# Sums of the output projection over 128 partitions, and kv joined with the next batch's projections, in a fused attention-and-FFN kernel

## The chip, the cores and the metric

The kernel runs on one core of one Trainium2 chip, in fp32. The metric is the device time of one execution in microseconds (us). The core's engines run side by side and wait for each other by semaphores: PE (TensorE, matrix products), ACT (ScalarE), DVE (VectorE), POOL (GpSimd) and SP (SyncE, which here only issues DMAs).

## The reference

An attention with squared sketches as features is followed by a gated feed-forward network. The attention's output is its input.

```python
batch, n_heads, seq, head_dim = (4, 4, 1088, 32); r = 8
def phi(x):
    a = np.einsum('rd,bhsd->bhsr', S1, x)
    b = np.einsum('rd,bhsd->bhsr', S2, x)
    return np.einsum('bhsi,bhsj->bhsij', a, b).reshape(*x.shape[:-1], r * r)
q_p, k_p = (phi(q), phi(k))
kv = np.einsum('bhsf,bhsd->bhfd', k_p, v)
z = np.sum(k_p, axis=2)
num = np.einsum('bhsf,bhfd->bhsd', q_p, kv)
den = np.einsum('bhsf,bhf->bhs', q_p, z)[..., None] + 1e-06
x = (num / den).transpose(0, 2, 1, 3).reshape(B * S, H * D)   # 4352 x 128
gate = 1.0 / (1.0 + np.exp(-(x @ w_gate)))                    # 128 -> 1536
return gate * (x @ w_val) @ w_out                             # 1536 -> 128
```

## The kernel before

**The feed-forward network in slots.** The 4352 tokens are cut into nine chunks of 512 (the last has 256). The 1536 hidden columns are twelve blocks of 128. One *slot* of the program handles one block of one chunk, in the last chunk two blocks, so slots are numbered through: slots 0 to 11 are the first chunk, 12 to 23 the second. In a slot, `w1` multiplies the tokens by a block of `w_gate` and `w_val` (a *wave*: eight matmuls, line 540) into one of two PSUM buffers "wave". ACT takes the sigmoid (`sg`, line 548), and at the beginning of the next slot `glu` has DVE multiply (`g`, line 583). The buffer is free for the wave after next when `g` is written. Where a wave buffer is also taken by an attention group (`qcomp`, `parts`), the ring moves by one.

**Seven products instead of eight.** In the seven full chunks after the first, two blocks of `g` (a pair: an even and an odd slot) are multiplied by `w_out` in the manner of Strassen and Winograd: the token dimension is halved (HALF = 256), `token_sums` (line 367, on POOL) forms differences `t[:, 0..3]` of the quarters of the pair, `weight_sums` (line 363) once those of the weights (`ws`), and seven products of 64×256 (`product`, line 377) take the place of eight. Two products run side by side on the two column halves of TensorE. For an odd slot n, `w2_a` with four products is due in slot n+3 and `w2_b` with three in slot n+4. They accumulate over the six pairs of a chunk in two PSUM banks, `acc0` and `acc1`, one for each function. After the sixth pair the partial sums are added: ACT copies what a sum needs from PSUM (lines 473 and 502), DVE adds (`add`, line 479) and transposes (line 514), SP stores.

**The queues of the order.** `moe["todo"]` holds the products with the slot in which they are due; `moe["late"]` holds closing work of a chunk, of which `slot()` takes one item per slot behind `glu`. Then come the products that are due, and then `w1`. The order of PE, DVE, ACT and POOL is the order in which the program is written; that of the DMA issues on SP is set by a scheduler. An engine does its instructions in that order.

**The attention between the slots.** Batch 0 and the first weights are handled ahead of and in the first slots. The work of batches 1 to 3 is put between slots by hand; for 2 and 3, `plan` lists the slot of each step:

- `turn_k`, `turn_q` (DVE transposes), then in `begin` the projections `kps` of k and `qcomp` of q (TensorE), whose result `spread` writes to DRAM and reads back spread over the partitions into `qp`, `bq`, and in small pieces `a` and `b` (SP).
- `outer` (DVE, the features of k, line 752), `sum_z` (DVE, lines 926 ff.), `kv` (TensorE, 36 small matmuls at line 892 and four at 901) and its copy `kvd` (ACT, line 914).
- `weights_z` (three DVE instructions from line 1001), `ndt` (line 957), `qmult` (DVE, the features of q, line 872), and `parts`: `den_j` (line 1021), numerators `nps` (line 1258), `den_i` (line 1034), whose quotient goes into `xT`, the tokens of the next waves.

`kps`, `kvz` and the second part of the numerators, `nps2`, take turns in one PSUM buffer "two". `load_kq` and `load_v` load the inputs of a batch. `kq` and `bq` take turns in buffers of the pool `ld`.

Of the kernel before, what the change touches and what calls it, by code (L numbers as in the profile page):

```python
# [8 lines left out]
F32 = mybir.dt.float32  # L9
# [7 lines left out]
P = 128  # L17
# [3 lines left out]
def kernel(  # L21
# [34 lines left out]
    sbN = ctx.enter_context(tc.tile_pool(name="sbN", bufs=1))  # L56
    sbG = ctx.enter_context(tc.tile_pool(name="sbG", bufs=3))

# [207 lines left out]

    def new_kq(b):
        t = ld.tile([P, 2 * H * W1], F32, tag="kq", name="kq")
        kq = t[:, : 2 * T * D].rearrange("p (a t d) -> p a t d", a=2, t=T)
        k_t[b], q_t[b] = kq[:, 0], kq[:, 1]  # L270
# [76 lines left out]
    moe = {"sum": -1, "ci": 0, "w": 0, "n": 0, "ready": 0, "acc": None, "gate": None, "todo": [], "late": []}  # L347
# [17 lines left out]
    def token_sums(g, t, odd):  # L365
        def sub(u, in0, in1):
            nc.gpsimd.tensor_tensor(out=t[:, u], in0=in0, in1=in1, op=ALU.subtract)  # L367

        if not odd:
            sub(0, g[:, 0, HALF:], g[:, 0, :HALF])  # L370
            return
        sub(2, g[:, 1, HALF:], t[:, 0])
        sub(3, t[:, 2], g[:, 1, :HALF])
        sub(1, g[:, 1, HALF:], g[:, 0, HALF:])

    def product(out, lhsT, rhs, start, stop):
        nc.tensor.matmul(  # L377
            out=out, lhsT=lhsT, rhs=rhs, start=start, stop=stop, skip_group_check=True
        )
# [34 lines left out]
    def w2(ci, j0, jn, g):  # L414
        if j0 == 0:
            moe["sum"] = ci
            moe["acc"] = pso.tile([P, TCH], F32, tag="acc0", name="moeout")
        for jj in range(jn):
            j = j0 + jj
            for d in (slice(0, P),) if j < NJ - 2 else (slice(0, 64), slice(64, P)):  # L420
                nc.tensor.matmul(  # L421
                    out=moe["acc"][d],
                    lhsT=w_sb[:, 2, j, d],
                    rhs=g[:, jj],
                    start=(j == 0),
                    stop=(j == NJ - 1),
                )
        if j0 + jn == NJ:
            o_sb = sbA.tile([P, 2, TCH // 32, 32], F32, tag="o_sb", name="o_sb")[:, 0]
            nc.vector.transpose(out=o_sb.rearrange("p t d -> p (t d)"), in_=moe["acc"])  # L430
            moe["store"] = lambda: store(
                ci, lambda g4: o_sb[32 * g4 : 32 * g4 + 32], nc.scalar
            )
# [25 lines left out]

    def w2_a(ci, i, g, t):  # L460
        if i == 0:
            moe["sum"] = ci
            fst["a"] = pso.tile([P, TCH], F32, tag="acc0", name="prod")
        lo, hi = fst["a"][:64], fst["a"][64:]
        w, first, last = w_sb[:, 2], i == 0, i == NJ // 2 - 1
        product(lo[:, :HALF], w[:, 2 * i, :64], g[:, 0, :HALF], first, last)
        product(hi[:, :HALF], w[:, 2 * i + 1, :64], g[:, 1, :HALF], first, last)
        product(lo[:, HALF:], ws[:, 3, i], g[:, 1, HALF:], False, last)
        product(hi[:, HALF:], ws[:, 1, i], t[:, 2], False, last)
        if last:  # L470
            e = fst["e"] = raw.tile([P, 2, 2, HALF], F32, tag="w_in", name="other")[:64]
            r = fst["r"] = raw.tile([P, 6, HALF], F32, tag="w_in", name="res")[:64]
            nc.scalar.copy(out=e[:, 0], in_=hi.rearrange("p (u x) -> p u x", u=2))

            add(ends(r, 1, 3), twice(lo[:, :HALF]), e[:, 0])
            moe["late"] += [lambda: add(r[:, 2], lo[:, HALF:], r[:, 4])]

    def add(out, in0, in1, op=ALU.add):
        nc.vector.tensor_tensor(out=out, in0=in0, in1=in1, op=op)  # L479

    def twice(x):
        return bass.AP(tensor=x.tensor, offset=x.offset, ap=[list(x.ap[0]), [0, 2], [1, HALF]])

    def ends(r, u, step):
        x = r[:, u]
        return bass.AP(
            tensor=x.tensor, offset=x.offset, ap=[list(x.ap[0]), [step * HALF, 2], [1, HALF]]
        )

    def w2_b(ci, i, g, t):  # L490
        if i == 0:
            fst["b"] = pso.tile([P, TCH], F32, tag="acc1", name="prod")
        lo, hi = fst["b"][:64], fst["b"][64:]
        w, first, last = w_sb[:, 2], i == 0, i == NJ // 2 - 1
        p5 = (lo[:, :HALF], ws[:, 0, i], t[:, 0], first, last)
        p4 = (hi[:, :HALF], w[:, 2 * i + 1, 64:], t[:, 3], first, last)
        p7 = ((hi if i % 2 else lo)[:, HALF:], ws[:, 2, i], t[:, 1], False, i >= NJ // 2 - 2)
        for p in (p4, p5, p7) if i % 2 else (p5, p4, p7):
            product(*p)
        if last:  # L500
            e, r = fst["e"], fst["r"]
            nc.scalar.copy(out=e[:, 1], in_=hi.rearrange("p (u x) -> p u x", u=2))
            o_sb = sbA.tile([P, 2, TCH // 32, 32], F32, tag="o_sb", name="o_sb")

            def fifth_seventh():
                add(ends(r, 2, 3), twice(lo[:, :HALF]), ends(r, 2, 2))
                add(r[:, 0], lo[:, HALF:], e[:, 1, 1])

            def last_sums():
                add(r[:, 3], r[:, 4], e[:, 1, 0], op=ALU.subtract)  # L510
                add(r[:, 3:5], ends(r, 3, 2), twice(r[:, 0]))

            def turned(d):
                nc.vector.transpose(  # L514
                    out=o_sb[:64, d].rearrange("p t x -> p (t x)"),
                    in_=r[:, 1 + 2 * d : 3 + 2 * d].rearrange("p u x -> p (u x)"),
                )

            def turn_store():
                turned(1)  # L520
                store(ci, lambda g4: o_sb[32 * (g4 % 2) : 32 * (g4 % 2) + 32, g4 // 2])

            moe["late"] += [fifth_seventh, last_sums, lambda: turned(0), turn_store]

    def w1():
# [40 lines left out]
        if ci == 1 and j0 == 1:  # L566
            weight_sums(NJ // 4, NJ // 2)
# [4 lines left out]
        def glu():  # L572
# [19 lines left out]
            if odd:  # L592
                part = (ci, j0 // 2, pair, moe["t"])
                early = ci == len(tok_chk) - 2 and j0 == NJ - 1
                todo.append((n + 3 - early, lambda: w2_a(*part)))
                todo.append((n + 4 - early, lambda: w2_b(*part)))
# [13 lines left out]
    def slot(group, waves, behind=None):  # L610
# [4 lines left out]
        for _ in range(waves):  # L615
# [12 lines left out]
            if more:  # L628
                w1()
            elif not todo:  # L630
                break
            else:
                todo.pop(0)[1]()
# [29 lines left out]
    def kps(b):  # L663
        t = ps2.tile([P, 2, 512], F32, tag="two", name="kps")
        ts = [t[:, 0], t[:, 1]]
# [168 lines left out]
    def spread(b, ns, cq, put, get):  # L834
# [19 lines left out]
        B8[b] = sbA.tile([P, W1], F32, tag="b8", name="b8", bufs=1)  # L854
        A8[b] = sbA.tile([P, 2, WD], F32, tag="a8", name="a8", bufs=1)
# [32 lines left out]
    def kv(b, zsum):  # L888
        kvz = KVZ[b] = ps2.tile([P, 2, 512], F32, tag="two", name="kvz")[:, 0]
# [264 lines left out]
    warm(64)  # L1154
# [77 lines left out]
    def begin(b):  # L1232
        glu()
        kps(b)
        cq[b] = qcomp(b, (0, 1), (psm, "wave"))
        spread(b, (0, 1), cq[b], nc.scalar, nc.sync)
# [7 lines left out]
    def part01(first):  # L1244
        glu()
        late.append(dn(0, 1)(first=first, later=True))
# [19 lines left out]
    def parts(b):  # L1266
# [6 lines left out]
        nc.scalar.copy(out=num, in_=t)  # L1273
        t = ps2.tile([P, 2, 512], F32, tag="two", name="nps2")
        numerators(b, t[:, :, WD : WD + 32], True)
        turn_den(b, den_i(b, t[:, 0, :WD]))
        for n in range(2):
# [33 lines left out]
    slot(lambda: part01(lambda: narrow_w(NJ - 1, 3)), 1)  # L1311
    slot(last01, 1)
    load_v(1)
    turn_k(1)
# [19 lines left out]
    load_kq(2)  # L1334
# [7 lines left out]
    plan = {2: (27, 29, 30, 31, 32, 34, 36, 37, 38, 39, 42, 44)}  # L1342
    plan[3] = (48, 49, 51, 53, 56, 57, 58, 59, 60, 61, 63, 68)
    for b in range(2, B):
        at = iter(plan[b])
        until(next(at))
        turn_k(b)
        for n in range(2):
            until(next(at))
            turn_q(b, n)  # L1350
        until(next(at))
        slot(lambda: begin(b), 1)
        for pi in range(2):
            until(next(at))
            outer(b, pi)
        for step in range(2):
            until(next(at))
            sum_z(b, step)
        until(next(at))
        slot(lambda: kv_all(b), 1)  # L1360
        if b + 1 < B:
            load_v(b + 1)
        until(next(at))
        qmult(b, 0)
        slot(lambda: ndt(b), 1)
        weights_z(b)
        until(next(at))
        qmult(b, 1)
        load_kq(b + 1)
        until(next(at))  # L1370
        slot(lambda: parts(b), 1)
# [31 lines left out]
```

## Time and profile before

| | |
|---|---|
| median of 3 runs | 292.99 us (292.74 to 293.36) |
| profiled execution | 296.02 us; span 294.1 us |
| granted TensorE clock | 0.999 of full |
| busy PE / DVE / POOL / ACT | 288.8 / 186.5 / 160.6 / 93.7 us |
| waves, line 540 | 820 matmuls, 210.6 us |
| products, line 377 | 588 matmuls, in four groups of 62.8, 34.7, 25.3 and 25.0 us |
| sums of the products on DVE, line 479 | 35 instructions, 24.9 us; transposes at line 514: 14, 9.6 us |
| token sums on POOL, line 367 | 168 instructions, 134.8 us |

The profile is of one execution and its times are in us; the span is from the first to the last instruction, and the execution's time is 1.92 us more. An engine's busy time says how long it had work, not that anything waited for it. Ends of matmuls are modelled, so the distance between two starts is the safer reading. Matmuls on two halves of the array run side by side, so their busy times add up to more than the engine's. In a line of the timeline stand the start, the duration, the engine, the line of the program, the operation, output and inputs by name, and in square brackets the idle time of the engine just before, with what ended it; a number behind x at the end is that of instructions joined in the line. In the groups, the output's and the input's partitions and elements are given as 128x256.

### The profile page before, as it was taken

What the parts mean: (1) busy time and instruction counts of PE and PEld (TensorE: products, weight loads), DVE (VectorE), ACT (ScalarE), POOL (GpSimd) and SP (SyncE); (2) the same over time, 40 slices, a digit from 0 to 9 for tenths busy, and PEclk for the clock granted to TensorE, in tenths of its full rate; (3) what the DMA queues carried; (4) which work ended last, traced back from release to release, by engine and by line L of the source; (5) the groups of instructions that cost most, each with busy time, mean ns of one, the idle gap of its engine ahead of it and who ended that gap; (6) DMA issues with size and microseconds to landing.
All of it is one profiled execution on the core that took longest, in us unless ns stands there. A gap on an engine that the chain in (4) does not pass through costs nothing.

```text
span 294.1 us, 5762 instructions
## 1 busy us (share of the span) xinstructions
PE 288.8 (98%) x2264; PEld 156.6 (53%) x2264; DVE 186.5 (63%) x316; ACT 93.7 (32%) x172; POOL 160.6 (55%) x222
## 2 busy tenths in 40 slices
PE   8989999999999999999999999999999999999995
PEld 3543433355455455545555555554555555555895
DVE  5778789885656766677556696667436423552482
ACT  3386542321324222323224222323223223322321
POOL 2266544796535657655456498555456565646300
PEclk9999999999999999999999999999999999999999
DMA  7993613295640168416000474202000200020003
GB/s 219 347 336 68 150 39 125 74 180 137 186 97 0 19 163 159 133 50 177 12 0 2 129 174 106 37 0 38 1 0 2 36 2 0 0 31 7 0 4 54
DMA packets 28890, 24.23 MB, mean 82 GB/s; under 512 B 18560, under 2 KB 24064, under 8 KB 28864
## 3 DMA queue, kind: packets, MB, share of 16 engines
q1 hardware_dynamic: 25808, 21.95, 30.1%
q10 hardware_dynamic: 3056, 1.92, 2.3%
q8 instruction: 18, 0.29, 0.4%
q14 instruction: 8, 0.07, 0.1%
HBM read 20.60 MB, written 3.26 MB: 81 GB/s over the span
## 4 chain that ended last, share of the span: by engine, by line
PE 89%; DMA 7%; SPq 1%; DVE 0%; issue 0%; ACT 0%; DVEq 0%
PE wave L540 55%; PE prod L377 20%; DMA bq<-dq 5%; PE moeout L421 4%; PE moeout L447 2%; PE warm L297 1%; PE kps L673 1%; SPq L844 1%; PE nps L1258 1%; DMA s_in<-in_S_dram 1%; PE kvz L892 1%; PE cqps L819 1%; DMA dq<-cq 1%; DMA b<-dq 1%; PE denj L1021 0%; PE dps L1063 0%
## 5 line engine op out<-in xcount | busy, mean ns | idle before, releaser
L540 PE MATMUL wave<-xT,w_sb 128*64 128x512 f32 (+3 forms) x820 | 210.6, 566 | 0.0
L540 PEld LDWEIGHTS wave<-xT,w_sb 128*64 128x64 f32 (+1 forms) x820 | 85.4, 140 | 63.2 <-issue 51.0
L548 ACT ACTIVATE sg<-wave 128x512 f32<-128x512 f32 x102 | 60.9, 597 | 171.1 <-PE wave L540 163.2
L583 DVE TENSOR_TENSOR g<-wave,sg 128x512 f32<-128x512 f32 x96 | 65.9, 686 | 76.3 <-ACT sg L548 75.0
L367 POOL TENSOR_TENSOR tsum<-g 128x256 f32<-128x256 f32 x84 | 67.9, 810 | 29.7 <-DVE g L583 29.6
L367 POOL TENSOR_TENSOR tsum<-g,tsum 128x256 f32<-128x256 f32 x42 | 34.2, 814 | 57.8 <-DVE g L583 57.6
L377 PE MATMUL prod<-tsum,ws 128*64 128x256 f32 x252 | 62.8, 381 | 0.0
L377 PEld LDWEIGHTS prod<-tsum,ws 128*64 128x64 f32 x252 | 31.2, 137 | 16.0 <-issue 11.8
L377 PE MATMUL prod<-g,w_sb 128*64 128x256 f32 x168 | 34.7, 381 | 0.0
L367 POOL TENSOR_TENSOR tsum<-tsum,g 128x256 f32<-128x256 f32 x42 | 32.7, 779 | 3.3
L377 PE MATMUL prod<-tsum,w_sb 128*64 128x256 f32 x84 | 25.3, 383 | 0.0
L377 PEld LDWEIGHTS prod<-g,w_sb 128*64 128x64 f32 x168 | 16.0, 136 | 17.5 <-issue 14.7
L377 PE MATMUL prod<-g,ws 128*64 128x256 f32 x84 | 25.0, 379 | 0.0
L117 POOL TENSOR_TENSOR head<-head,tail 128x384 int32<-128x384 int32 (+1 forms) x10 | 9.9, 987 | 13.9 <-DVE head L111 12.6
L377 PEld LDWEIGHTS prod<-g,ws 128*64 128x64 f32 x84 | 11.5, 137 | 3.7
L421 PE MATMUL moeout<-g,w_sb 128*128 128x512 f32 (+1 forms) x28 | 12.5, 603 | 0.0
L377 PEld LDWEIGHTS prod<-tsum,w_sb 128*64 128x64 f32 x84 | 10.8, 137 | 3.0 <-issue 2.2
L872 DVE TENSOR_TENSOR qp<-qp,bq 128x1152 f32<-128x1152 f32 (+1 forms) x7 | 9.4, 1344 | 4.6 <-DMA a<-dq 4.6
L752 DVE TENSOR_TENSOR kp<-kab 128x1152 f32<-128x1152 f32 (+2 forms) x10 | 10.9, 1101 | 0.0
L576 DVE TENSOR_TENSOR g<-wave,sg 128x512 f32<-128x512 f32 x6 | 6.7, 1121 | 4.6 <-ACT sg L548 4.6
L479 DVE TENSOR_TENSOR res<-prod,other 64x512 f32<-64x512 f32 (+1 forms) x14 | 7.6, 544 | 3.1 <-DMA a<-dq 1.6
L514 DVE STREAM_TRANSPOSE o_sb<-res 64x512 f32<-64x512 f32 x14 | 9.6, 688 | 0.0
(129 smaller groups left out, 209.6 us busy)
## 6 DMA issues: line engine op xcount, KB each, us to landing
qp<-dq SPq DMA_DIRECT2D x7, 576.0 KB
bq<-dq SPq DMA_DIRECT2D x14, 288.0 KB
kq<-in_k_dram SPq DMA_DIRECT2D x3, 544.0 KB
kq<-in_q_dram SPq DMA_DIRECT2D x3, 544.0 KB
w_in<-in_moe_w_out_dram SPq DMA_DIRECT2D x6, 256.0 KB
w_in<-in_moe_w_gate_dram SPq DMA_DIRECT2D x5, 256.0 KB
w_in<-in_moe_w_val_dram SPq DMA_DIRECT2D x5, 256.0 KB
v<-in_v_dram SPq DMA_DIRECT2D x8, 144.0 KB
```

Of the source, the lines that this page charges most:

```text
L117: nc.gpsimd.tensor_tensor(out=head, in0=head, in1=tail, op=ALU.add)
L367: nc.gpsimd.tensor_tensor(out=t[:, u], in0=in0, in1=in1, op=ALU.subtract)
L377: nc.tensor.matmul(out=out, lhsT=lhsT, rhs=rhs, start=start, stop=stop, skip_group_check=True)
L421: nc.tensor.matmul(out=moe["acc"][d], lhsT=w_sb[:, 2, j, d], rhs=g[:, jj], start=(j == 0), stop=(j == NJ - 1),)
L479: nc.vector.tensor_tensor(out=out, in0=in0, in1=in1, op=op)
L514: nc.vector.transpose(out=o_sb[:64, d].rearrange("p t x -> p (t x)"), in_=r[:, 1 + 2 * d : 3 + 2 * d].rearrange("p u x -> p (u x)"),)
L540: nc.tensor.matmul(out=wv[d, which, jj * tw + o : jj * tw + o + tp], lhsT=w_sb[:, which, j0 + jj, d], rhs=xT[:, t0 + o : t0 + o + tp], sta ...
L548: nc.scalar.activation(out=sg, in_=wv[:, 0], func=ACTF.Sigmoid)
L576: nc.vector.tensor_tensor(out=g.rearrange("p (j u s y) -> p j y u s", j=2, u=2, y=4), in0=wv[:, 1].rearrange("p (j y u s) -> p j y u s", j ...
L583: nc.vector.tensor_tensor(out=g, in0=wv[:, 1], in1=sg, op=MUL)
L752: eng.tensor_tensor(out=KP[b][:, pi, j0:j1].rearrange("p j m (i l) -> p (j m) i l", i=R), in0=bass.AP(tensor=a0.tensor, offset=a0.offset, ...
L872: nc.vector.tensor_tensor(out=q0, in0=q0, in1=half(BQ[b], n), op=MUL)
```

## The change

**Sums over 128 partitions.** In `w2_a` and `w2_b` the products are put into the halves of the banks in another way, so that DVE adds whole 128-partition rows of 256 elements. The product of `g[:, 1, :HALF]` with `w_out` moves from `w2_a` to `w2_b`, that of `t[:, 1]` from `w2_b` to `w2_a`; the sign of `t[:, 3]` is turned, and `token_sums` writes 1 ahead of 3. ACT copies 64×256 seven times per chunk; a new list `moe["copies"]` holds copies that are issued behind the slot's `w1`. The closing sums are five, the transpose is one, and `late` gets two items per chunk where it got five.

**kv joined.** `begin(b, also)` and `parts(b, also)` take the `kv` of a batch into their own group: `kv(2)` is written into the buffer of `kps(3)` ahead of it, `kv(3)` into that of `nps2(2)`. Its copy `kvd` goes to `copies`. Batch 3 so begins before batch 2 has ended.

**Order.** Batch 2 begins in slot 27 (it was 31), batch 3 in slot 36 (53) and ends in slot 56 (68). `weights_z(2)` stands in slot 37 ahead of `outer(3, 0)` and of that slot's `glu`. `kq` of batches 2 and 3 lies in a pool of its own, opened once that of the weight narrowing is closed; `load_kq(2)` follows `load_v(1)`, `load_kq(3)` follows `turn_q(2, 1)`. The second part of `weight_sums` comes in slot 11 (13), the `early` products of the last full chunk come when the others do, and the start's `warm` matmul has 128 columns (64).

```diff
     def token_sums(g, t, odd):
...
         sub(2, g[:, 1, HALF:], t[:, 0])
-        sub(3, t[:, 2], g[:, 1, :HALF])
         sub(1, g[:, 1, HALF:], g[:, 0, HALF:])
+        sub(3, g[:, 1, :HALF], t[:, 2])
...
     def w2_a(ci, i, g, t):
...
         product(lo[:, :HALF], w[:, 2 * i, :64], g[:, 0, :HALF], first, last)
-        product(hi[:, :HALF], w[:, 2 * i + 1, :64], g[:, 1, :HALF], first, last)
+        product(hi[:, :HALF], ws[:, 1, i], t[:, 2], first, last)
         product(lo[:, HALF:], ws[:, 3, i], g[:, 1, HALF:], False, last)
-        product(hi[:, HALF:], ws[:, 1, i], t[:, 2], False, last)
+        product(hi[:, HALF:], ws[:, 2, i], t[:, 1], False, last)
         if last:
...
-            nc.scalar.copy(out=e[:, 0], in_=hi.rearrange("p (u x) -> p u x", u=2))
-            add(ends(r, 1, 3), twice(lo[:, :HALF]), e[:, 0])
-            moe["late"] += [lambda: add(r[:, 2], lo[:, HALF:], r[:, 4])]
+            nc.scalar.copy(out=e[:64, 0], in_=hi[:, :HALF])
+            nc.scalar.copy(out=e[64:, 0], in_=lo[:, :HALF])
+            add(r[:, 0], ps[:, :HALF], e[:, 0])
+            add(r[:, 0], ps[:, HALF:], r[:, 0])
+            moe["copies"] += [
+                lambda: nc.scalar.copy(out=e[:64, 1], in_=lo[:, :HALF]),
+                lambda: nc.scalar.copy(out=e[64:, 1], in_=r[64:, 0]),
+            ]
...
     def w2_b(ci, i, g, t):
...
-        p5 = (lo[:, :HALF], ws[:, 0, i], t[:, 0], first, last)
+        p5 = (lo[:, HALF:], ws[:, 0, i], t[:, 0], False, last)
         p4 = (hi[:, :HALF], w[:, 2 * i + 1, 64:], t[:, 3], first, last)
-        p7 = ((hi if i % 2 else lo)[:, HALF:], ws[:, 2, i], t[:, 1], False, i >= NJ // 2 - 2)
-        for p in (p4, p5, p7) if i % 2 else (p5, p4, p7):
+        out2 = hi[:, HALF:] if i % 2 else lo[:, :HALF]
+        p2 = (out2, w[:, 2 * i + 1, :64], g[:, 1, :HALF], first, i >= NJ // 2 - 2)
+        for p in (p4, p5, p2) if i % 2 else (p2, p4, p5):
             product(*p)
...
+            add(r[:, 1], ps[:, :HALF], e[:, 1])
+            add(r[:64, 1], r[:64, 1], e[:64, 3])
...
+            moe["late"] += [lambda: add(r[:, 2], r[:, 0], e[:, 2]), turn_store]
...
     def slot(group, waves, behind=None):
...
                 w1()
-            elif not todo:
+            for copy in moe["copies"]:
+                copy()
+            moe["copies"] = []
...
-    def kps(b):
+    def kps(b, also=None):
         t = ps2.tile([P, 2, 512], F32, tag="two", name="kps")
+        if also is not None:
+            kv(also, ZS[also], t[:, 0, NJK * 32 : NJK * 32 + 2 * F])
...
-    def begin(b):
+    def begin(b, also=None):
         glu()
-        kps(b)
+        kps(b, also)
+        if also is not None:
+            moe["copies"].append(lambda: kvd(also))
...
-    def parts(b):
+    def parts(b, also=None):
...
-        nc.scalar.copy(out=num, in_=t)
+        first = t
         t = ps2.tile([P, 2, 512], F32, tag="two", name="nps2")
         numerators(b, t[:, :, WD : WD + 32], True)
+        if also is not None:
+            kv(also, ZS[also], t[:, 1, 4 * F : 6 * F])
+        nc.scalar.copy(out=num, in_=first)
         turn_den(b, den_i(b, t[:, 0, :WD]))
+        if also is not None:
+            moe["copies"].append(lambda: kvd(also))
...
-    plan = {2: (27, 29, 30, 31, 32, 34, 36, 37, 38, 39, 42, 44)}
-    plan[3] = (48, 49, 51, 53, 56, 57, 58, 59, 60, 61, 63, 68)
...
+    until(24)
+    turn_k(2)
+    until(25)
+    turn_q(2, 0)
+    until(26)
+    turn_q(2, 1)
+    load_kq(3)
+    until(27)
+    slot(lambda: begin(2), 1)
+    features(2, 28, 29, 31, 32)
+    until(34)
+    turn_k(3)
+    until(35)
+    turn_q(3, 0)
+    turn_q(3, 1)
+    until(36)
+    slot(lambda: begin(3, 2), 1)
+    load_v(3)
+    until(37)
+    weights_z(2)
+    outer(3, 0)
+    until(38)
+    slot(lambda: ndt(2), 1)
+    outer(3, 1)
+    until(40)
+    qmult(2, 0)
+    until(41)
+    sum_z(3, 0)
+    until(42)
+    sum_z(3, 1)
+    until(44)
+    qmult(2, 1)
+    until(45)
+    slot(lambda: parts(2, 3), 1)
+    until(48)
+    weights_z(3)
+    slot(lambda: ndt(3), 1)
+    until(50)
+    qmult(3, 0)
+    until(52)
+    qmult(3, 1)
+    until(56)
+    slot(lambda: parts(3), 1)
     slot(None, 10**3)
```

`features` calls `outer(b, 0)`, `outer(b, 1)`, `sum_z(b, 0)` and `sum_z(b, 1)` at the slots given.

## The prediction, on record before the changed kernel ran

> **What bounds the kernel now.** I read the page first: busy time, the row of slices, then the shares of the chain.
>
> ```profile
> PE 288.8 (98%) x2264; PEld 156.6 (53%) x2264; DVE 186.5 (63%) x316; ACT 93.7 (32%) x172; POOL 160.6 (55%) x222
> PE   8989999999999999999999999999999999999995
> PE 89%; DMA 7%; SPq 1%; DVE 0%; issue 0%; ACT 0%; DVEq 0%
> ```
>
> TensorE works in every slice, and the chain that ended last is 89% TensorE. So work on another engine counts only where TensorE waits for it, and such a wait must be looked up in the timeline. There, four slots (four waves of eight matmuls, two groups of four and two of three products) take 9.89 us: 1.72 a wave, .86 four products, .645 three. Subtracting these from the distances between the starts of successive TensorE groups leaves about 17.6 us after slot 12; 13.8 of it are the attention's own matmuls (per batch kps .51 and cqps .62, kv 1.03 and .23, ndps .22, denj .30, nps 1.09, den_i .32), which the change keeps. The rest is what a change of order can win. Two kinds are in the timeline. The first, in slots 28 and 29:
>
> ```profile
> 94.39 1.88 PE L540 MATMUL wave<-xT,w_sb 128*64 128x512 f32 x7
> ...
> 95.56 0.41 DVE L479 TENSOR_TENSOR res<-prod,other 64x256 f32<-64x256 f32 x1
> ...
> 96.11 0.40 PE L377 MATMUL prod<-tsum,ws 128*64 128x256 f32 x1
> ```
>
> The next chunk's first `w2_b` product starts .14 us after the last DVE sum that reads bank `acc1` (95.97). From the wave's seven remaining records to the product 1.72 us pass (94.39 to 96.11); with no wait it is about 1.33. Second, the attention groups:
>
> ```profile
> 118.05 1.94 PE L540 MATMUL wave<-xT,w_sb 128*64 128x512 f32 x8
> 119.92 1.21 PE L892 MATMUL kvz<-kp,v 128*32 128x64 f32 x72
> 121.31 0.37 ACT L914 COPY kvd<-kvz 128x256 f32<-128x256 f32 x1 [0.69 <-PE kvz L901]
> ```
>
> The wave ahead of a group of another tile shape takes 1.87 us start to start (118.05 to 119.92) instead of 1.72: .15 for the change of shape.
>
> POOL has 45% idle, but is not free at will:
>
> ```profile
> 180.76 1.22 DVE L872 TENSOR_TENSOR qp<-qp,bq 128x1024 f32<-128x1024 f32 x1
> 180.99 1.57 POOL L367 TENSOR_TENSOR tsum<-g,tsum 128x256 f32<-128x256 f32 x1 [0.97 <-DVE g L583]
> 182.64 0.73 POOL L367 TENSOR_TENSOR tsum<-tsum,g 128x256 f32<-128x256 f32 x1
> ```
>
> The same subtraction takes .73 us alone and 1.57 beside a DVE product of two SBUF tensors: it ends .58 after that one.
>
> **What the skill says.** The Trainium skill, "SBUF — State Buffer", section "SBUF: two separate sides", says that DVE and GpSimd share a port pair under an exclusive lock: a DVE instruction with two SBUF inputs holds it, and a GpSimd instruction that reads SBUF waits. The three lines above agree (1.57 against .73). "TensorEngine Tiling (Array Packing)", "Key Properties", says that a change of tiling mode drains TensorE; the .15 us agrees. "PSUM — Partial Sum Buffer", "Specifications (TRN2)", allows a VectorE instruction one tensor input from PSUM; hence the ACT copies between the sums, which the trace shows (L473, L502) without proving the rule.
>
> **The change, part by part.**
>
> *Sums over 128 partitions.* DVE per chunk before: five L479 sums, 3.56 us (24.9 over seven chunks), and two transposes of .69, 4.9 in all. After: five sums at .41 and one transpose of .69, 2.75. DVE is 63% busy and not the bound, so these 2.2 us count only through the banks. `acc0` is now read last by the two sums right after `w2_a(5)`: two copies of .37, the wait of .25, two sums of .41 with .25 for the start, some 3.0 to 3.2 us after its last product; wanted after two waves and three products, 2·1.72+.645 = 4.09. `acc1` comes free about 5.7 us after `w2_a(5)`, wanted at 6.7. **The bank waits go**: .39 in each of slots 29 and 41, about .1 in each of three later chunks, less what they had covered. Between 1.14 and .6; I take **−.88**. ACT gets seven copies of .37 (2.6 us) for two of .58, 1.4 more per chunk, under a wait for waves of over 1 us ahead of most sigmoids: nothing. If that cover is gone, a sigmoid is late by .37.
>
> *Order of products and token sums.* The count stays seven per pair. `w2_a` now needs `t[:,2]` in its second product and `t[:,1]` in its fourth; before, `t[:,2]` in its fourth alone. From the end of the odd wave, t2 is ready after .25+.60+.69+.15+.73 = 2.4 us and t1 at 3.1; wanted at about 5.0 and 5.4 (.86+1.72+.645+1.72, and half of four products more). So some 2.4 us are left: none in steady running, but two locked subtractions in a row (.84 each) and a late `g` use them up.
>
> *kv joined.* `kv(2)` is followed by `kps(3)` and `kv(3)` stands between `nps2` and the denominators. Their shapes differ (128\*32, 64\*32), so three changes remain of four at each place: 2 × .14 = **−.28** (0 to −.4). `kvd` moves behind the slot's sigmoid on ACT; see below.
>
> *Starts and transfers.* `warm(128)`: about +.05 (0 to .1), most of it under the first loads. `load_kq(2)` passes ahead of `spread(1)` on SP. It needs the memory of the closed pool, free when DVE's last narrowing ends (46.6); kq(1) moved the same bytes in about 4 us and the DMA engines are idle from 48 to 54, spread(1) issues at 56.7: nothing, up to .3 if it is late. `load_kq(3)` goes to slot 26, where SP has batch 2's spread behind it: 1.1 MB, long landed at slot 34's `turn_k(3)` (before, 4 us sufficed). `v(3)` is issued ahead of batch 3's spread, `bq(3)` behind four stores and `qmult(2,1)`; their landings, by some slot 40 and 47, precede `sum_z`/kv at 45 and `qmult(3,0)` at 50. Removing `early` and the second `weight_sums` two slots sooner: nothing, POOL idle there (5 us before 53.29).
>
> *Batch 1, slot 16.* t1 of pair (12,13) is now wanted at 59.6; POOL's two subtractions there took 1.85 and 1.65 us under DVE's kp and z (57.44, 59.37), so it is ready near 60.6. But batch 1 waits at slot 22 anyway, about .87 us for the `b` load (76.79, released by DMA), at a time set by SP. TensorE arriving later waits less there: **+.15** (0 to .6).
>
> *Slots 36 to 44*, the new crowding. Clock at the start of wave 36. Sigmoid 36 ends at 2.57 (1.72+.25+.60). Only then ACT copies `kvd(2)`: 2.97. DVE has `weights_z(2)` next in its order: .7 to 1.05 us (rows .22 to .63, .22, .22 to .46), then `outer(3,0)`, 1.3; only then `g` of wave 36. It ends at 5.7 to 6.2. Wave 38 writes into wave 36's buffer. TensorE gets there after 1.72+.645+1.72+.3 (ndps)+.86 = 5.25. So a stall of .3 to 1.05: **+.7**. Behind it stand two sums, `outer(3,1)`, two sums, `qmult(2,0)` 1.3, the late sum, `sum_z` 1.3, the transpose, `sum_z` 2.5 and `qmult(2,1)` 1.3 in eight slots: about 11.3 us (sums .41, transpose .69) besides eight `g` of .61 (4.9), 16.2 in 8 × 2.47 = 19.8 us, and in bunches. By that order `g` 41 ends near 18.3, .3 late for wave 43, and the lock of `qmult(2,1)` keeps t2 of pair (40,41) until 20.75 and t1 until 21.45, so `w2_a` in slot 44 waits .8. Together **+1.1** (0 to 1.5).
>
> After slot 46 DVE's load falls; batch 3's denominators at slot 56 have eight slots after `weights_z(3)`, and the tail is the same: nothing.
>
> Sum: −.88 −.28 +.05 +.15 +.7 +1.1 = **+.84 us**. Against the profiled execution (span 294.1, run 296.02, of which 1.92 lies outside the span) that is a span of 294.9 and a run of 296.9. The median of the runs, 292.99, is 3.0 lower; applied to it: **293.8 us**. A measurement here tells about 0.2%, .59 us: no change is 292.4 to 293.6.
>
> **Rivals.**
> A, *the stalls don't come, and it is faster.* Decisive: `g` 36 done 5.1 us after wave 36 starts. For it: `weights_z` with its short rows is .66, DVE has 37% idle, and before it was hardly a releaser. Against: the order on DVE is fixed, and kvd behind the sigmoid is arithmetic. Time: 292.99−.88−.28+.05 = 291.9.
> B, *only wave 38 stalls*; the delay it makes gives POOL and DVE the time they lack later. 292.99−1.11+.15+.7 = 292.7.
> C, *the lock bites more widely, slower still*: t2 and t1, wanted earlier everywhere, also come late where DVE's sums of batch 2 (slots 28 to 32) and batch 1 run: +.6 at slot 16 unabsorbed and +.6 around slot 32. 293.8+1.2 = 295.0. It decides where two locked subtractions meet a `g` late by .8.
> That the joined kv saves nothing since the shapes still differ is a rival to −.28 alone; it is in the range.
>
> **Numbers.** Forecast .38 (.30 slower, .08 same); A .24 (.22 faster, .02 same); B .16 (.05, .10, .01 slower); C .22. Faster .27, same .20, slower .53. Both signs hold weight: the forecast's own range is 293.2 to 294.6; the whole, with A and C and the ends of the unknowns (−1.5 to +2.65 in sum, neither likely), 291.7 to 295.4.
>
> **What would show it.** Right: no wave of 1.7 for seven records in slots 29 and 41, the sums in rows of 128x256 near .41; `g` of wave 36 ending over 5.3 us after its wave's start, and wave 38 released by it; `w2_a` of slot 44 released by POOL. Wrong: wave 38 at the streaming rate (A), product waits on POOL at slots 31 to 33 (C), or TensorE waiting for a DMA at batch 1, 2 or 3 beyond the .87 of before.

## The result: 0.27% slower, and the profile after

The kernel after takes 293.75 us (median of 22 runs), the kernel before 292.99 us (median of 22): ratio 1.0027, interval 1.0020 to 1.0035. That is .76 us more, a little over what a measurement here can tell. The prediction was 293.8 us, slower. Ratios here and below are taken from the fast runs of a kernel and of the kernel before in the same series (one run of the kernel after, of 297.79 us, was a slow one), and so they differ a little from the quotient of the medians given.

The page of the profile after, in the same three views as before (busy time; TensorE in the forty slices; the chain by engine):

```profile
PE 286.1 (98%) x2264; PEld 159.8 (55%) x2264; DVE 174.6 (60%) x302; ACT 102.2 (35%) x207; POOL 158.9 (54%) x222
PE   8899999999999999999999999999999999999995
PE 96%; POOL 1%; ACT 1%; DVE 1%; issue 0%; POOLq 0%
```

DVE has 12 us less work, ACT 8 us more, and TensorE is still the bound. What is new is POOL in the chain with 1%: the products now wait for it.

The span of this profile, 292.2 us, is 1.9 us shorter than that of before, although the runs are longer. The cause lies ahead of the end of the first slot, which comes at 16.67 us and not at 18.98. Here are the first projections of batch 0 in the first profile of before (timeline, TensorE):

```profile
6.30 1.21 PE L673 MATMUL kps<-kT,sk 64*32 64x288 f32 x16
7.44 1.16 PE L780 MATMUL aps<-qT,s 32*64 32x256 f32 x16
```

and in a second profile of the same program, in the same view:

```profile
5.73 0.72 PE L673 MATMUL kps<-kT,sk 64*32 64x288 f32 x16
6.77 0.69 PE L780 MATMUL aps<-qT,s 32*64 32x256 f32 x16 [0.32 <-DVE qT L653]
```

The same matmuls take 1.21 and .72 us. The Trainium skill, "TensorE: Matmul & The Clock Gate", "Part 1: The HAM clock gate (the "warmup" mystery)", says that a TensorE not busy long enough runs at half clock, and that when it changes depends on the phase of a free-running window and so on the run. Two executions of one program whose matmuls differ by a factor of 1.7 would fit that, but the factor is not 2, and the profile gives a granted clock of 1.00 between 6 and 10 us in both; so no trace here shows the gate at work, and what made the start slow stays open. From here on the second profile of before (span 291.3 us, run 293.05) stands for before.

To compare, I took in every profile the distance between the last wave matmuls of successive slots, subtracted the streaming time of the waves and products in it, and summed that from slot 12. This "excess" holds the attention's matmuls and all waits. The profiles are one execution each; between two with the same order the slots agree within about .01 us, except slots 22 and 45, whose waits vary (see below). (us)

| slots | before | new sums, old plan | after |
|---|---|---|---|
| 12 to 26 | 6.01 | 6.36 | 6.36 |
| 27 to 72 | 10.77 | 10.20 | 11.37 |
| 73 to the end | .67 | .49 | .49 |
| sum | 17.45 | 17.05 | 18.22 |

The sum rises by .77 us from before to after, the medians by .76. That the two agree so closely is chance, since slots 22 and 45 differ by some tenths from one profile to the next. The middle column is an experiment below: in these profiles the new sums alone win .40 us, and the new plan loses 1.17.

Where the bank waits were, in slots 28 and 29 (timeline of after; DVE's sums are line 492, `w2_b`'s products line 381):

```profile
92.08 0.42 DVE L492 TENSOR_TENSOR res<-res,other 64x256 f32<-64x256 f32 x1
...
93.36 1.88 PE L542 MATMUL wave<-xT,w_sb 128*64 128x512 f32 x7
...
94.70 0.59 PE L381 MATMUL prod<-g,w_sb 128*64 128x256 f32 x2
```

From seven records of the wave to the product 1.34 us pass, where 1.72 passed. Of the wait nothing is left.

And the place that made POOL appear, slot 16 of batch 1 (timeline of after; `tsum` are POOL's differences, in the order t2, t1, t3):

```profile
54.66 1.35 DVE L760 TENSOR_TENSOR kp<-kab 128x1152 f32<-128x1152 f32 x1
54.89 1.71 POOL L371 TENSOR_TENSOR tsum<-g,tsum 128x256 f32<-128x256 f32 x1 [3.19 <-DVE g L585]
...
56.53 1.22 DVE L937 TENSOR_TENSOR z<-kp 128x1024 f32<-128x1024 f32 x1
56.57 1.76 POOL L371 TENSOR_TENSOR tsum<-g 128x256 f32<-128x256 f32 x1
...
58.38 0.43 PE L381 MATMUL prod<-tsum,ws 128*64 128x256 f32 x1 [0.71 <-POOL tsum L371]
```

Two differences in a row start just after a DVE instruction with two SBUF inputs and last 1.7 us; t1 is done at 58.33, and `w2_a`'s fourth product follows at 58.38.

### The profile page after: what moved, and what is told of

Read it like the earlier page. It is cut to its first block, busy times and chain, and to the rows that moved or that the text cites. A ratio compares the mean times of both kernels' runs of the same rounds, so it can differ in the third digit from the quotient of the medians.

```text
span 292.2 us, 5780 instructions
## 1 busy us (share of the span) xinstructions
PE 286.1 (98%) x2264; PEld 159.8 (55%) x2264; DVE 174.6 (60%) x302; ACT 102.2 (35%) x207; POOL 158.9 (54%) x222
## 4 chain that ended last, share of the span: by engine, by line
PE 96%; POOL 1%; ACT 1%; DVE 1%; issue 0%; POOLq 0%
PE wave L542 60%; PE prod L381 21%; PE moeout L425 4%; PE warm L301 2%; PE moeout L451 2%; POOL tsum L371 1%; PE nps L1271 1%; PE kps L681 1%; PE cqps L827 1%; PE nps L1093 0%; PE denj L1032 0%; PE nps L1045 0%; PE dps L1074 0%; PE nps L903 0%; PE kvz L888 0%; PE kvz L903 0%
## 5 line engine op out<-in xcount | busy, mean ns | idle before, releaser
L371 POOL TENSOR_TENSOR tsum<-g,tsum 128x256 f32<-128x256 f32 x84 | 69.8, 831 | 66.5 <-DVE g L585 66.2
L371 POOL TENSOR_TENSOR tsum<-g 128x256 f32<-128x256 f32 x84 | 65.5, 779 | 27.1 <-DVE g L585 26.9
L381 PE MATMUL prod<-tsum,ws 128*64 128x256 f32 x252 | 69.1, 381 | 0.7 <-POOL tsum L371 0.7
L381 PE MATMUL prod<-g,w_sb 128*64 128x256 f32 x168 | 50.1, 380 | 0.0
L381 PEld LDWEIGHTS prod<-tsum,ws 128*64 128x64 f32 x252 | 32.5, 137 | 10.4 <-issue 5.5
L381 PEld LDWEIGHTS prod<-g,w_sb 128*64 128x64 f32 x168 | 22.8, 137 | 22.8 <-issue 20.0
L881 DVE TENSOR_TENSOR qp<-qp,bq 128x1152 f32<-128x1152 f32 (+1 forms) x7 | 10.2, 1464 | 1.5 <-DMA bq<-dq 1.5
L492 DVE TENSOR_TENSOR res<-prod,other 128x256 f32<-128x256 f32 x14 | 5.9, 424 | 4.0 <-ACT other L483 2.2
L301 PE MATMUL warm<-const-float32-1.0 128*128 128x512 f32 (+2 forms) x12 | 7.2, 729 | 0.8 <-PEq L1426 0.8
L425 PEld LDWEIGHTS moeout<-g,w_sb 128*128 128x128 f32 (+1 forms) x28 | 4.1, 174 | 6.1 <-issue 3.7
```

The source lines that it names most:

```text
L301: nc.tensor.matmul(out=t[:, 0, :n], lhsT=x, rhs=r, start=True, stop=True)
L381: nc.tensor.matmul(out=out, lhsT=lhsT, rhs=rhs, start=start, stop=stop, skip_group_check=True)
L425: nc.tensor.matmul(out=moe["acc"][d], lhsT=w_sb[:, 2, j, d], rhs=g[:, jj], start=(j == 0), stop=(j == NJ - 1),)
L492: nc.vector.tensor_tensor(out=out, in0=in0, in1=in1, op=ALU.add)
L881: nc.vector.tensor_tensor(out=q0, in0=q0, in1=half(BQ[b], n), op=MUL)
```

## The experiments

**The start.** The kernel before once more (no edit), the kernel after with `warm(64)`, the kernel before with `warm(128)`:

```diff
-    warm(128)
+    warm(64)
```

> The kernel before, unchanged, profiled once more. In its first profile the projections of batch 0 (16 matmuls) took 1.14 us and the 512-column warm pair 1.87; in the kernel after .65 and about 1.07. Theory S (the first profile fell into a start at half TensorE clock, which its other runs don't have): the projections now take about .65 us, the first slot's end moves from 18.98 us to about 16.6, and the run comes out near 293.0. Rival (every run of the kernel before starts so): 18.98 again, and a run near 296.

> The kernel after with warm(64) as before. Theory: .05 us less work ahead of the projections, so 0 to .1 us faster than the kernel after on most runs, and the start of half clock in some of them, 2 us or more longer. Rival (the missing .4 us between the traces and the medians is the warm matmul's): .3 to .5 us faster, a ratio to before of about 1.0012.

> The kernel before with warm(128). Theory: 0 to .1 us slower than before (ratio 1.0000 to 1.0004). Rival (it costs .4 us): ratio 1.0014.

Measured: before again 293.05 us, the first slot's end at 16.50 us instead of 18.98. After with `warm(64)`: 293.76 us, ratio to before 1.0031 (1.0020 to 1.0042), the same as after. Before with `warm(128)`: 292.75 us, ratio .9992 (.9975 to 1.0009). The `warm` matmul is worth nothing that can be measured; the slow start came in one profiled execution of before and didn't come in the second. That 128 columns would prevent it is not shown.

**The sums alone.** The kernel after with the old plan: `features` and the list of slots after it are replaced by the old `plan` and its loop.

```diff
     load_v(1)
-    load_kq(2)
...
     qmult(1, 1)
+    load_kq(2)
...
-    until(24)
-    turn_k(2)
...
+    plan = {2: (27, 29, 30, 31, 32, 34, 36, 37, 38, 39, 42, 44)}
+    plan[3] = (48, 49, 51, 53, 56, 57, 58, 59, 60, 61, 63, 68)
```

> The kernel after with the old plan: batches 1 to 3 begin, run their kv and end in the slots of the kernel before, kv in groups of its own, load_kq(2) where it was. The new sums, products, token sums, copies, warm(128), the weight sums' place and the products without the early ones stay. Theory (the sums gain, the plan loses): the bank waits of slots 29, 41, 65, 77 and 89 (.42, .41, .05, .09, .10 over streaming) are gone, 1.0 us; slot 16 loses .93 and slot 22 gives .58 of it back, so -.65 us against before, ratio near 0.9978. Rival (the new order of products loses more than its banks gain, at other slots with batch 2's and 3's sums): ratio 1.000 to 1.002.

Measured: 292.63 us, ratio 1.0006 (.9988 to 1.0025), so the runs don't tell whether the sums alone gain; in the profiles the excess falls by .40 us (17.45 to 17.05). It consists of +.35 up to slot 26 and −.75 after: .41 around slot 29 and .09 each around slots 41, 65, 77 and 89. At slot 41 the wait itself had lasted .40 too; what it cost there was mostly made up in slot 43.

**Slot 16.** In the kernel after, the products of the first pair are due one slot later; and the same with the old plan.

```diff
-                todo.append((n + 3, lambda: w2_a(*part)))
-                todo.append((n + 4, lambda: w2_b(*part)))
+                wait = 1 if n == 13 else 0
+                todo.append((n + 3 + wait, lambda: w2_a(*part)))
+                todo.append((n + 4 + wait, lambda: w2_b(*part)))
```

> The kernel after with the first pair's products (pair of slots 12 and 13) due one slot later each. Theory (they wait for t2 and t1, which POOL gets late beside DVE's features of batch 1, .93 us; the kernel before waited .58 us for a DMA at slot 22, which this delay hides): slots 16 and 17 lose nothing, slot 22 takes 4.96 us instead of 4.38, and the time falls by .35 us, ratio near 1.0015. Rival 1 (the delay at slot 16 is paid in full): slot 22 stays at 4.38, .9 us faster, ratio 0.9995. Rival 2 (all of it is absorbed): no change, 1.0027.

> Both together: new sums, old plan, first pair's products one slot later. Theory: -.65 -.35 = -1.0 us against before, ratio 0.9966. Rival (slot 22's DMA then waits by as much as slot 16 did): 0.9978, as without the edit.

Measured: the kernel after so changed takes 293.17 us, ratio 1.0011 (.9999 to 1.0022); the excess up to slot 26 falls from 6.36 to 5.44 us, all of the .92. Slot 22 stayed at 4.38 us, so in this execution rival 1 was right. With the old plan it is 292.02 us, ratio .9977 (.9969 to .9986), faster than before; in its profile slot 22 took 4.97 us. I took the early `load_kq(2)` for the difference and tried it:

```diff
     load_v(1)
+    load_kq(2)
     turn_k(1)
...
     qmult(1, 1)
-    load_kq(2)
```

> New sums, old plan, first pair's products one slot later, and load_kq(2) right behind load_v(1) as in the kernel after. With the first three, slot 22 waited for a DMA again (4.97 us); in the kernel after with the first pair later it did not (4.38). Theory (the early load_kq(2) shifts which transfer the last b of batch 1 has to wait for, and so takes that wait away): slot 22 takes 4.38 us, .58 us faster than without this edit, near 291.4 us, ratio 0.9957. Rival (another part of the new plan took the wait away): 4.97, 292.0 us, ratio 0.9977.

Measured: 292.02 us, ratio .9964 (.9950 to .9978); slot 22 took 4.38 us. But this edit tells nothing on `load_kq(2)`: the scheduler had issued it at that place already (27.65 us after the end of the first slot in the kernel without the edit, 27.64 with it), and the order on SP is the same in both. So these are two executions of the same order, one with the wait at slot 22 and one without (in that with the wait the first slot ended 5 us late). What varies is when the last `b` of batch 1 is issued: 16.4 to 18.2 us after the batch's first `qp` in the profiles of all these kernels. TensorE waits for it where it arrives soon after that. In the kernels with slot 16's delay (six profiles) it arrives about 2 us or more after that issue, and never waited. Without the delay it arrived .92 us earlier and lost .58 to .98 us there in three of three profiles of kernels with the old sums, 0, 0, 0, .15 and .59 in five with the new ones. So the delay is absorbed by as much as the DMAs happen to be late: .58 between the profiles that I compare. Whether the new order of loads makes them come sooner stays open.

That it is DVE's instruction which holds POOL up:

```diff
+    def outer_copy(b, pi):
...
+        nc.scalar.copy(
...
-        outer(1, pi)
+        (outer_copy if pi else outer)(1, pi)
```

> The kernel after in which the second features of batch 1, outer(1,1), are replaced by a copy on ACT of their first factor: it leaves out the product with the second factor, and takes 1.35 us with two SBUF inputs off DVE at 54.66. Theory (DVE's instruction holds the port that POOL needs): the subtractions at 54.89 and 56.57 take about .73 instead of 1.71 and 1.76, t1 is ready by 57, and slot 16 takes 2.5 us, not 3.52. Rival (POOL is late since g is, or the products wait for something else): slot 16 keeps 3.5.

Measured: 292.65 us in one run; slot 16 takes 2.59 us instead of 3.52. The timeline of POOL in this kernel:

```profile
54.49 0.73 POOL L371 TENSOR_TENSOR tsum<-g,tsum 128x256 f32<-128x256 f32 x1 [3.18 <-DVE g L585]
55.17 0.74 POOL L371 TENSOR_TENSOR tsum<-g 128x256 f32<-128x256 f32 x1
55.86 0.74 POOL L371 TENSOR_TENSOR tsum<-g,tsum 128x256 f32<-128x256 f32 x1
56.55 1.72 POOL L371 TENSOR_TENSOR tsum<-g 128x256 f32<-128x256 f32 x1
```

With that instruction off DVE the first three differences take .73 us; the fourth starts beside DVE's sum `z` (56.41 to 57.68) and takes 1.72. Shown, then: the differences are late because of the DVE instructions beside them. All of these have two SBUF inputs.

**kvd behind the sigmoid.** In `begin`, kvd is issued at once:

```diff
         if also is not None:
-            moe["copies"].append(lambda: kvd(also))
+            kvd(also)
         cq[b] = qcomp(b, (0, 1), (psm, "wave"))
```

> The kernel after with kvd(2) issued on ACT in begin itself, ahead of the spread's copy and of the sigmoid of slot 36, so that weights_z(2) and outer(3,0) on DVE are done before the sigmoid is. Theory (kvd behind the sigmoid makes g of slot 36 late and TensorE wait .4 to .55 us for it in slot 38): g of slot 36 ends 3.3 us after its wave starts, not 5.4, slot 38 lasts 2.55 instead of 2.97, and the time falls by .3 to .5 us, ratio near 1.0013. Rival (the later slots 42 to 46 take it back, since DVE and POOL set the pace there): slots 42 to 46 longer by as much, no change, ratio 1.0027.

Measured: 293.45 us, ratio 1.0010 (.9998 to 1.0022). In the timeline of after, ACT, DVE and TensorE in slots 36 to 38 (wave 36 starts at 115.66):

```profile
118.10 0.37 ACT L925 COPY kvd<-kps 128x256 f32<-128x256 f32 x1
...
118.50 0.23 DVE L1012 TENSOR_TENSOR zz<-kvd,unit 128x64 f32<-128x64 f32 x1 [3.21 <-ACT kvd L925]
118.76 0.22 DVE L1018 TENSOR_REDUCE z<-zz 128x8 f32<-128x64 f32 x1
119.01 0.22 DVE L1019 TENSOR_TENSOR zw<-z,eight 128x64 f32<-128x64 f32 x1
119.15 1.35 DVE L760 TENSOR_TENSOR kp<-kab 128x1152 f32<-128x1152 f32 x1
...
120.42 1.28 DVE L585 TENSOR_TENSOR g<-wave,sg 128x512 f32<-128x512 f32 x2
...
121.16 1.94 PE L542 MATMUL wave<-xT,w_sb 128*64 128x512 f32 x8
```

DVE is idle 3.21 us until kvd, then all follows as in the prediction, and wave 38 starts .06 us after the first of the two `g` (1.28 for both, so about 121.1). In the edited kernel the `g` of slot 36 runs here (timeline):

```profile
115.34 0.37 ACT L925 COPY kvd<-kps 128x256 f32<-128x256 f32 x1 [2.31 <-DVE kab L691]
...
118.27 0.69 DVE L585 TENSOR_TENSOR g<-wave,sg 128x512 f32<-128x512 f32 x1 [0.40 <-ACT sg L550]
```

It ends 3.3 us after its wave's start. Slot 38 takes 2.80 us instead of 2.97, not the 2.55 that was expected. The excess up to slot 44 falls from 11.47 to 11.11: the wait is worth .36 us, .22 in slots 38 and 39 and .13 in slot 42. The later slots did not take it back.

**The two joins.** kv(2) in a group of its own in slot 35, kv(3) in one of its own in slot 44:

```diff
+    slot(lambda: kv_all(2), 1)
     until(36)
-    slot(lambda: begin(3, 2), 1)
+    slot(lambda: begin(3), 1)
```

> The kernel after with kv(2) in a group of its own in slot 35, kvd(2) behind it at once, and begin(3) alone in slot 36. To be compared with the kernel after with kvd(2) ahead of the copy, in which kvd is early too but kv joined. Theory (joining saves one change of shape there, and no pause was seen in that group): slots 34 to 39 sum to .14 to .2 us more than there; time 293.5. Rival (the join saves nothing): the same sum, time 293.3 to 293.4.

```diff
     qmult(2, 1)
+    slot(lambda: kv_all(3), 1)
     until(45)
-    slot(lambda: parts(2, 3), 1)
+    slot(lambda: parts(2), 1)
```

> The kernel after with kv(3) in a group of its own in slot 44 instead of inside parts(2) in slot 45, and its kvd at once. Theory (joining saves one change of shape, .14, and costs a pause of up to .36 us ahead of the end of wave 45, seen in one profile of two): the same within .2 us; slots 44 to 46 sum to the same. Rival 1 (the join is what it says, .15 to .3 cheaper): slower by .15 to .3, ratio 1.0034. Rival 2 (the join costs, since TensorE runs out of instructions in the long group): faster by .3, ratio 1.0017.

Measured, kv(2) alone: 293.65 us, ratio 1.0017 (1.0000 to 1.0034). Up to slot 40 the excess is 10.95 against 10.75 us with kv joined and kvd early: joining saves .20 there. kv(3) alone: 293.34 us, ratio 1.0027 (1.0011 to 1.0042), which by itself decides nothing; its excess up to slot 47 is 14.67 us, against 15.34 in the kernel after and 14.98 in the kernel after with `warm(64)`, whose order there is the same. So in the profiles this join costs .31 to .66 us. Where it is lost can be seen in the timeline of TensorE in the kernel after (the group, and wave 45 behind it):

```profile
138.29 0.50 PE L1032 MATMUL denj<-b,zw 64*32 64x160 f32 x16
138.59 1.16 PE L1271 MATMUL nps<-qp,nd 64*32 64x512 f32 x32
139.74 1.21 PE L903 MATMUL nps<-kp,v 128*32 128x64 f32 x72
...
141.75 0.59 PE L542 MATMUL wave<-xT,w_sb 128*64 128x512 f32 x1
...
142.18 2.21 PE L542 MATMUL wave<-xT,w_sb 128*64 128x512 f32 x6
...
144.23 0.59 PE L542 MATMUL wave<-xT,w_sb 128*64 128x512 f32 x1
```

in the kernel after with `warm(64)`:

```profile
138.19 0.50 PE L1032 MATMUL denj<-b,zw 64*32 64x160 f32 x16
...
141.68 0.59 PE L542 MATMUL wave<-xT,w_sb 128*64 128x512 f32 x1
...
142.11 1.81 PE L542 MATMUL wave<-xT,w_sb 128*64 128x512 f32 x6
...
143.75 0.59 PE L542 MATMUL wave<-xT,w_sb 128*64 128x512 f32 x1
```

and with kv(3) alone:

```profile
141.38 0.59 PE L542 MATMUL wave<-xT,w_sb 128*64 128x512 f32 x1
...
141.81 1.88 PE L542 MATMUL wave<-xT,w_sb 128*64 128x512 f32 x7
```

From the start of its first record to that of its last, wave 45 takes 2.48 us in the first, 2.07 in the second and 1.71 with kv(3) alone (the last of the seven starts at 143.10). In all six profiles of kernels with this join, one half of TensorE begins its third record .30 to .85 us later than at the wave's pace; in five of them the other half comes to stand still as well (in the kernel after, both until 143.75), and nothing that the profile shows is waited for. In the two profiles with kv(3) apart there is no such pause. In the trace's DMA records a block of 16 KB of instructions begins to come 2.86 to 3.29 us after the start of the group in the six, and TensorE goes on 2.2 to 2.5 us after the block began. This speaks for TensorE running out of instructions behind a group of 132 small matmuls; it was not tried apart, and the group of 112 in slot 36 has no pause. Apart from the pause the joined group is some .05 to .1 us shorter than the two groups.

**Together.** The three edits that helped the kernel after:

> The kernel after with the three edits that helped it one by one: kvd(2) ahead of the spread's copy, the first pair's products one slot later, kv(3) alone in slot 44. Theory (they concern three different waits): the excess over streaming falls by .92 + .5 + .5 from 18.2 to about 16.3 us, the time to 292.0, ratio 0.9972. Rival (they hide each other): 292.7 or more.

Measured: 292.10 us, ratio .9978 (.9961 to .9995), excess 16.41 us. The effects add up (18.22 − .92 − .36 − .66 = 16.28, and .15 was lost at slot 22). So these waits are most of what the new plan had lost. The old plan with the new sums and the first pair one slot later does as well without the new order: .9977 and .9964 in two comparisons, 292.02 us in both, about .7 to 1 us faster than the kernel before. Its intervals and that of .9978 overlap, so the runs don't tell which of the two is faster.

## Why the prediction was right, by its steps

The sign and the size were as forecast: the sum was +.84 us; the excess rose by .77. The mechanism was right in part. DVE and POOL crowded by the new order did make TensorE wait at slot 16 and at wave 38, but hardly at slots 42 to 44, where the largest term stood. Two costs that the prediction didn't have took its place: a pause behind the joined kv(3), and a dearer place for `begin(3)`. That the sum came out all the same is to that extent luck.

- **Bank waits, −.88 taken: −.75.** They went, as forecast, in every slot named. The term was counted too high at slot 41, where .40 of wait cost .09.
- **kv joined, −.28 taken: −.20 for kv(2), and +.31 to +.66 for kv(3)** (.66 in the profile compared here). The step "three changes remain of four at each place" held at the first. At the second the wave behind the long group pauses, a price that the step didn't have.
- **Slot 16, +.15 taken: +.35.** The lock came as worked out (t1 forecast some 1 us late, .93 measured), and so did its absorption at slot 22. The term was mis-sized since the first profile of before showed an absorbable wait of .87, and the second had .58.
- **Wave 38, +.7 taken: +.36.** The chain kvd, `weights_z`, `outer`, `g` is there row by row; `weights_z` took .73 us, near the low end of .7 to 1.05, and `g` ended 5.4 us after its wave's start, over the 5.3 named as a sign but under the forecast of 5.7 to 6.2.
- **Slots 42 to 44, +1.1 taken: about +.2**, of which .13 went with the late kvd. Slots 42 and 43 last 5.32 us against 5.10 with the new sums and the old plan, and slot 44 lasts 2.58, with nothing waited for. This was the worst step. The stall of `w2_a` in slot 44 did not come. The timeline of after shows why (DVE's `qmult(2, 1)` is line 881):

```profile
133.82 0.74 POOL L371 TENSOR_TENSOR tsum<-g,tsum 128x256 f32<-128x256 f32 x1 [1.02 <-DVE g L585]
...
134.51 0.74 POOL L371 TENSOR_TENSOR tsum<-g 128x256 f32<-128x256 f32 x1
134.55 1.91 DVE L881 TENSOR_TENSOR qp<-qp,bq 128x1152 f32<-128x1152 f32 x1
...
135.19 1.85 POOL L371 TENSOR_TENSOR tsum<-g,tsum 128x256 f32<-128x256 f32 x1
```

`qmult` starts .04 us after t1 had started, so t2 and t1 came unlocked and only t3 was held, which `w2_a` doesn't need. The forecast had let `qmult` go first. Who starts first, here by a few hundredths, decides over the .8 us that the forecast had put there; that `qmult` ahead would have cost so much was not tried. Wave 43 does start just behind `g` of slot 41 (at 133.73, .06 after it), but slot 43 is only .06 us longer than with the old plan.

- **`begin(3)` in slot 36, nothing taken: about +.3.** What is left of the 1.17 after the joins and kvd (1.17 + .20 − .66 − .36 = .35) lies mostly here. With kv(2) apart, `begin(3)` lengthens slots 36 and 37 together by 1.65 us; `begin(2)` lengthens slot 27 by 1.33. The difference shows in slot 37, which takes 2.57 us and not 2.20. Why this place is dearer stays open.
- `warm(128)`, +.05 taken: nothing measurable.

Of the rivals, B ("only wave 38 stalls") was nearer to what happened in slots 36 to 44 than the forecast was, though its time, 292.7 us, was not. C was right on its mechanism at slot 16 and nowhere else; from slot 27 to 35 the excess is 1.39 us against 1.79 before, less by the bank wait of slot 29 and no more for POOL. A failed at its point: `g` of slot 36 was done after 5.4 us, not 5.1.

Three figures of the working were off, and none of them carries the result. The attention's eight groups as listed add up to 4.32 us a batch and 13.0 for three, not 13.8. The terms listed for `acc0` add up to 2.1 us, not 3.0 to 3.2; 2.1 was measured, from the start of the last product of `w2_a` at 86.71 to the end of the second sum at 88.83. DVE's work listed behind `outer(3, 0)` is 10.4 us and not 11.3, and `g` takes .69 us on the page of before and not .61; the total hardly changes, 16.0 instead of 16.2.

## What to carry to other kernels

A change that relieves one engine can still lose by its order: moving a product that needs a POOL result one place forward made POOL's lock by DVE a wait of TensorE, and one slot of delay for one pair took it away again. Where a new wait is hidden behind an old one, look how much the old one varies from execution to execution before counting on it, and profile the kernel before twice if its profiled time stands away from its median. Long groups of very small matmuls may cost more than their streaming time, so joining two of them is not free. And a forecast that comes out in sum has not been confirmed in its terms: here the largest was wrong by about .9 us.

## What the runs showed of the hardware that I had not expected

- One program's first matmuls ran at 1.21 and at .72 us per sixteen in two executions, at a granted clock that the profile gives as 1.00 in that stretch in both; the first slot ended 2.5 us later in the slow one.
- In all six profiles with kv(3) joined, one half of TensorE paused for .30 to .85 us in the wave behind the group of 132 small matmuls, until 2.2 to 2.5 us after a 16 KB block of instructions began to load, with no wait that the profile names; in the two with kv(3) apart it didn't.
- The time from a batch's first spread load to the issue of its last one varied between 16.4 and 18.2 us over the profiles, and was 16.65 and 17.92 us in two executions with the same order of DMAs.
